# Linear attention and a highway layer: the last tile in three column pieces, and other stores

## The chip, the cores and the metric

The kernel runs on one core of one Trainium2 chip. The metric is the device time in microseconds, as the median of several runs. The engines of a core work side by side and wait for one another through semaphores: TensorE (PE, matmuls into PSUM[...]), VectorE (DVE), ScalarE (ACT), GpSimd (POOL, which works from SBUF alone here) and SyncE (SP), which here only issues transfers. A transfer runs on 16 DMA engines, and whoever needs its data waits for its landing.

## What is computed

For each of 8 batches and 8 heads (576 tokens, 64 dimensions each), q is put through a softmax over its dimensions, k through a softmax over its tokens, and attention is linear: `kv = k_s^T v`, `x = q_s kv`. The heads side by side make 4608 tokens of 512 features, and these go through a highway layer:

```
H = maximum(x @ w_h, 0)
T = 1 / (1 + exp(-(x @ w_t + b_t)))
out = T * H + (1 - T) * x          # float32, 4608 x 512
```

## The kernel before

**Tiles.** The output is cut into 36 tiles of 128 tokens by 512 features. A batch has 9 rows of 64 tokens (token `9p + j`, with p the partition and j the row). Eight rows make four tiles of two rows each, partitions 0 to 63 holding one and 64 to 127 the other; the ninth rows of two batches together make one more tile. So tiles 8, 17, 26 and 35 are ninth-token tiles, and 35 is the last of all. Tiles 0 and 4 are worked in two halves at the start.

**One tile.** `xu` multiplies the transposed exp(q) with the batch's kv (L326, TensorE), which also gives the softmax sums; `rs` and `x` divide (L335, L341, VectorE); `xt` transposes x (L348, TensorE) and `xe` copies it to SBUF as float16 (L355, VectorE or ScalarE). `mh` multiplies it with half of `w_h` less half of the identity (L383), `mt` with `w_t` (L374), into banks `gps` and `tps`. The bias is put into `tps` ahead of that by `bw`: a copy by ScalarE (L364) or a small matmul (L366). Then `th` takes the tanh of half of the gate (L399, ScalarE), `dd` makes `d = max(h, -x/2)` (L403, VectorE), `uu` makes `u = (1 + tanh) d` (L416, VectorE), and `oo` adds x (L432, GpSimd in most tiles). In some tiles, called lifted, GpSimd does `uu` as a plain product (L414) and another sum `ee` (L408), which spares VectorE a step. `st` stores.

**One batch.** `ek` and `eq` take exponentials on ScalarE, `vc` casts v, `kv` multiplies (L258), `kr` and `kn` divide by the sums and write the result to SBUF (L270, L276), `qt` transposes exp(q) (L299) and `qc` copies that out of PSUM (L308). The two banks of pool `ps_x` serve in turn `kv` of a batch and `xu` of every tile but 0 and 4: who comes next waits until VectorE has read what is there.

**Order.** All of it is one list written out by hand, `ORDER`, of some 700 steps (`kind_tile_part`, with `:A`, `:D` or `:P` for the engine where there is a choice). Each engine runs its own steps in the order of this list, and waits where a step's data or buffer isn't there yet. `fill_n` puts n matmuls on zeros where TensorE would stand idle. SP issues loads and stores in list order too, each on one of eight semaphores in turn, so a transfer is issued once the one eight places before it has landed. Weights, bias and inputs come in float32; matmuls are in float16.

**Buffers that the change touches.** Pool `ld` has three landing buffers each for k, q and v. Pool `op` has three buffers for pairs of tiles (`o32`, two tiles stored together) and three for tiles stored alone (`o1`: tiles 8, 17, 26 and 31 to 35). In the last tile, `mt`, `th`, `uu` and `oo` go by two halves of 256 columns, all in one bank `tps`, one buffer `u16` and one buffer `o1`:

```
def columns(i, h):
    return slice(h * DM // 2, (h + 1) * DM // 2) if i == LAST else slice(0, DM)
```

Its four stores are shared between SP and ScalarE's queue. A stored pair writes two rows that are not neighbours, so each packet has 2048 bytes; ninth tokens are stored in two transfers of 64 partitions.

Of the kernel before, what the change touches and what calls it, by code (L numbers as in the profile page):

```python
# [8 lines left out]
FP32 = mybir.dt.float32  # L9
# [7 lines left out]
b_0 b_32 setuppool fill_16_turned setupdve k_0_2 q_0_0 k_0_0 v_0_0 v_0_2 q_0_4 w_h_0 bsplit w_h_2 fill_4_turned bp  # L17
w_t_0 bc eq_0_0 w_t_2 ek_0_3 ek_0_1 v_1_2 ek_0_0 ek_0_2 vc_0_1:D vc_0_0 k_1_0 fill_20_xu_0_0 kv_0_0 qt_0_0 vc_0_2:A
vc_0_3:D k_1_2 qc_0_0:A half kr_0_0 fill_2_xu_0_0 kv_0_1 kn_0_0 kr_0_1 fill_1_xu_0_0 xu_0_0 kn_0_1 eq_0_1 q_1_0 rs_0_0
fill_3_xu_0_1 xu_1_0 x_0_0 xu_0_1 qt_0_1 rs_0_1 rs_1_0 v_1_0 whc_0 xt_0_0 qc_0_1:A x_1_0 whd_1 q_1_4 x_0_1 whc_2 k_2_0  # L20
v_2_0 q_2_0 k_3_0 bw_1 bw_0 fill_5_mh_0_0 xt_0_1 xu_2_0 xe_0_1 rs_2_0 xe_0_0 whd_2 fill_1_mh_0_0 xt_1_0 eq_0_2 whd_0
whd_3 wtc_0 fill_1_mh_0_0 mh_0_0 x_2_0 mh_0_1 xe_1_0 xu_3_0 wtc_2:D mt_0_0 xt_2_0 rs_3_0 dd_0 mt_0_1 mt_1_0 x_3_0
th_0_0 xe_2_0 mh_1_0 uu_0_0 th_1_0 bw_2:A xt_3_0 mh_2_0 dd_1 ek_1_1 uu_1_0 ek_1_0 mt_2_0 xe_3_0:D ek_1_2 dd_2 bw_3
mt_3_0 th_2_0 vc_1_3 vc_1_2 oo_0_0 oo_1_0 ek_1_3 uu_2_0 mh_3_0 th_3_0 oo_2_0 eq_1_0 kv_1_1 dd_3 kr_1_1 vc_1_0:A vc_1_1
fill_2_qt_1_0 qt_1_0 uu_3_0 kn_1_1 kv_1_0 qc_1_0:A kr_1_0 kn_1_0 eq_1_1 st_1_0_1 st_1_0_0 v_3_0 q_3_0 bw_5
fill_1_xu_4_1 xu_4_1 rs_4_1 fill_2_xu_4_0 xu_5_0 x_4_1 rs_5_0 fill_1_xu_4_0 qt_1_1 x_5_0 xu_4_0 bw_4 qc_1_1:A rs_4_0
xt_5_0 x_4_0 fill_2_mh_5_0 xu_6_0 ek_2_2 ek_2_0 xe_5_0:D xt_4_0 mh_5_0 rs_6_0 xe_4_0:D x_6_0 qt_0_2 mt_5_0 dd_5 qc_0_2
oo_3_0 xt_4_1 xu_7_0 th_5_0 xe_4_1:D mh_4_0 rs_7_0 vc_2_2:A vc_2_0 mh_4_1 mt_4_0 mt_4_1 eq_1_2 xt_6_0 qt_1_2 th_4_0
xe_6_0 st_3_0_0 eq_2_0 st_3_0_1 eq_2_1 k_4_0 eq_2_2 v_4_0 uu_5_0 x_7_0 dd_4 kv_2_0 uu_4_0 mh_6_0 kr_2_0 qc_1_2 kn_2_0
bw_6 xt_7_0 qt_2_0 xe_7_0:D dd_6 xu_8_0 mt_6_0 bw_7:A rs_8_0 qc_2_0 mh_7_0 x_8_0 th_6_0 ek_3_0 xu_9_0 uu_6_0 xt_8_0  # L30
mt_7_0 rs_9_0 xe_8_0:D bw_8:A x_9_0 mh_8_0 th_7_0 dd_7 ek_3_2 xt_9_0 oo_5_0 oo_4_0 oo_6_0 mt_8_0 uu_7_0 dd_8 xe_9_0
oo_7_0 xu_10_0 qt_2_1 bw_9:A st_5_0_0 rs_10_0 mh_9_0 x_10_0 th_8_0 st_5_0_1 vc_3_0:A vc_3_2 uu_8_0 mt_9_0 q_4_0 dd_9
xt_10_0 oo_8_0 th_9_0 kv_3_0 xe_10_0:D qc_2_1:A uu_9_0 mh_10_0 kr_3_0 kn_3_0 qt_2_2 eq_3_0 k_5_0 xu_11_0 bw_10 mt_10_0
rs_11_0 qc_2_2:A x_11_0 bw_11:A dd_10 xt_11_0 th_10_0 qt_3_0 xe_11_0:D oo_9_0 xu_12_0 uu_10_0 qc_3_0:A mh_11_0 q_5_0
rs_12_0 oo_10_0 x_12_0 mt_11_0 eq_3_1 dd_11 xt_12_0 bw_12:A xu_13_0 ee_11 xe_12_0:D qt_3_1 th_11_0 rs_13_0 mt_12_0
ek_4_2 x_13_0 v_5_0 uu_11_0:P qc_3_1 xu_14_0 xt_13_0 eq_3_2 mh_12_0 rs_14_0 th_12_0 xe_13_0:D x_14_0 ek_4_0 qt_3_2
mh_13_0 dd_12 bw_13:A xu_15_0 oo_11_0 vc_4_0 uu_12_0 xt_14_0 st_7_0_0 vc_4_2:A mt_13_0 rs_15_0 xe_14_0:D oo_12_0
st_7_0_1 x_15_0 mh_14_0 bw_14:A st_10_0_1 dd_13 xt_15_0 st_10_0_0 kv_4_0 dd_14 xe_15_0 th_13_0 ee_14 mt_14_0 kr_4_0
bw_15:A kn_4_0 ee_13 k_6_0 eq_4_0 qc_3_2 xu_16_0 mt_15_0 rs_16_0 th_14_0 x_16_0 eq_4_1 qt_4_0 xu_17_0 qc_4_0 th_15_0
mh_15_0 rs_17_0 ek_5_2 q_6_0 x_17_0 xt_16_0 qt_4_1 xe_16_0:D bw_16 ek_5_0 dd_15 xu_18_0 xt_17_0 mh_16_0 rs_18_0 x_18_0  # L40
xe_17_0 bw_17:A qc_4_1 xu_19_0 v_6_0 xt_18_0 eq_5_1 mh_17_0 rs_19_0 x_19_0 eq_5_0 mt_16_0 xe_18_0 mt_17_0 th_16_0
qt_5_0 vc_5_2:A st_12_0_0 st_12_0_1 th_17_0 qc_5_0:A eq_5_2 uu_14_0:P uu_13_0:P uu_15_0:P ee_15 dd_16 oo_14_0:D
oo_13_0 vc_5_0 uu_16_0 mh_18_0 dd_17 kv_5_0 oo_15_0 uu_17_0 bw_18 oo_16_0 xt_19_0 kr_5_0 mt_18_0 kn_5_0 xe_19_0
oo_17_0 qt_5_2 xu_20_0 th_18_0 mh_19_0 rs_20_0 bw_19:A bw_20:A qc_5_2 x_20_0 qt_5_1 dd_18 xt_20_0 xu_21_0 qc_5_1:A
mt_19_0 ee_18 rs_21_0 xe_20_0:D x_21_0 ek_6_0 mh_20_0 uu_18_0:P dd_19 xu_22_0 eq_4_2 xt_21_0 th_19_0 rs_22_0 qt_4_2
q_7_0 mt_20_0 ee_19 xe_21_0:D st_14_0_1 bw_21:A x_22_0 st_14_0_0 mh_21_0 eq_6_0 dd_20 k_7_0 qc_4_2 v_7_0 uu_19_0:P
xu_23_0 th_20_0 xt_22_0 mt_21_0 rs_23_0 xe_22_0 x_23_0 oo_18_0 ek_6_2 uu_20_0 xu_24_0 xt_23_0 qt_6_0 rs_24_0 xe_23_0:D
vc_6_0 vc_6_2:A st_8_0_1 mh_22_0 x_24_0 st_16_0_0 dd_21 st_16_0_1 bw_22:A xt_24_0 oo_19_0 kv_6_0 xe_24_0:D th_21_0
qc_6_0 eq_6_2 mt_22_0 ee_21 bw_23:A kr_6_0 kn_6_0 mt_23_0 oo_20_0 dd_22 eq_7_0 xu_25_0 mh_23_0 rs_25_0 uu_21_0:P
th_22_0 x_25_0 eq_7_1 qt_7_0 dd_23 xt_25_0 oo_21_0 xu_26_0 bw_24:A mh_24_0 th_23_0 uu_22_0:P eq_6_1 mt_24_0 st_21_0_0  # L50
uu_23_0:P bw_25:A st_19_0_0 ek_7_2 st_19_0_1 st_8_0_0 th_24_0 eq_7_2 ek_7_0 vc_7_2:A qc_7_0 rs_26_0 x_26_0 xe_25_0:D
dd_24 xu_27_0 xt_26_0 qt_6_1 rs_27_0 x_27_0 mt_25_0 ee_23 xe_26_0:D qc_6_1 xu_28_0 mh_25_0 ee_22 uu_24_0 xt_27_0
rs_28_0 mh_26_0 xe_27_0:D vc_7_0 x_28_0 qt_7_1 dd_26 xt_28_0 bw_26:A kv_7_0 dd_25 th_25_0 xe_28_0 mt_26_0 oo_23_0
oo_22_0 kr_7_0 qc_7_1:A kn_7_0 mh_27_0 oo_24_0 uu_25_0 th_26_0 xu_29_0 mh_28_0 st_23_0_0 uu_26_0 bw_27:A st_23_0_1
rs_29_0 bw_28:A mt_27_0 st_21_0_1 x_29_0 st_17_0_1 dd_27 xu_30_0 st_17_0_0 th_27_0 xt_29_0 mt_28_0 rs_30_0 dd_28
xe_29_0 x_30_0 oo_25_0 oo_26_0 ee_27 qt_7_2 mh_29_0 th_28_0 uu_27_0:P bw_29:A uu_28_0 xt_30_0 xu_31_0 xe_30_0 mt_29_0
oo_28_0 rs_31_0 dd_29 bw_30:A mh_30_0 x_31_0 th_29_0 oo_27_0 xt_31_0 uu_29_0 xu_32_0 xe_31_0 mt_30_0 rs_32_0 oo_29_0
dd_30 bw_31:A mh_31_0 x_32_0 st_28_0_0 th_30_0 st_26_0_0 xt_32_0 st_25_0_1 xu_33_0 xe_32_0 mt_31_0 st_26_0_1 st_28_0_1
mh_32_0 th_31_0 qc_7_2 uu_30_0 rs_33_0 dd_31 x_33_0 bw_32:A qt_6_2 uu_31_0 xt_33_0 xu_34_0 xe_33_0 mt_32_0 dd_32
qc_6_2:A rs_34_0 mh_33_0 x_34_0 th_32_0 bw_33:A xt_34_0 uu_32_0 xu_35_0 xe_34_0 dd_33 mt_33_0 bw_34:A rs_35_0 oo_30_0  # L60
st_30_0_0 oo_31_0 st_31_0_0 oo_32_0 st_25_0_0 st_31_0_1 x_35_0 mh_34_0 st_30_0_1 th_33_0 xt_35_0 uu_33_0 mt_34_0
st_32_0_1 xe_35_0:D st_32_0_0 bw_35:A oo_33_0 dd_34 mh_35_0 th_34_0 mt_35_0 uu_34_0 st_33_0_0 mt_35_1 st_33_0_1 dd_35
th_35_0 oo_34_0 th_35_1 uu_35_0 uu_35_1 oo_35_0:P st_34_0_0 oo_35_1 st_34_0_1 st_35_1_1 st_35_0_0 st_35_0_1 st_35_1_0
# [4 lines left out]
def kernel(  # L68
# [13 lines left out]
    P = 128  # L82
# [7 lines left out]
    ld = pool("ld", 3)  # L90
    ekp = pool("ekp", 2)
# [5 lines left out]
    op = pool("op", 3)  # L97
    PS = bass.MemoryType.PSUM
# [12 lines left out]
    b32 = consts.tile([P, DM], FP32, name="b32")  # L111
# [10 lines left out]
    def once(name, make):  # L122
        if name not in T:
            T[name] = make()
        return T[name]
# [16 lines left out]
    def columns(i, h):  # L142
        return slice(h * DM // 2, (h + 1) * DM // 2) if i == LAST else slice(0, DM)
# [33 lines left out]
    def landing(which, b):  # L177
        return once(f"{which}32{b}", lambda: ld.tile([P, 4, NJ * D], FP32, tag=which, name=f"{which}32_{b}"))
# [115 lines left out]
    def qt(e, b, g):  # L294
        j0, j1 = GROUPS[g]
        t = q_bank(b, g)
        for j in range(j0, j1):
            for kk in range(2):
                nc.tensor.matmul(  # L299
                    t[:, (j - j0) // 2, 2 * kk:2 * kk + 2, (j - j0) % 2],  # L300
                    T[f"qe{b}"][:, j, 2 * kk:2 * kk + 2].rearrange("p c d -> p (c d)"), idh,
                    is_transpose=True, start=True, stop=True, skip_group_check=True)
# [55 lines left out]
    def gate_bank(i):  # L358
        return once(f"tps{i}", lambda: ps_t.tile([P, DM], FP32, tag="tps", name=f"tps_{i}"))

    def bw(e, i):
        t = gate_bank(i)
        if e == "A":
            nc.scalar.copy(t, ball)  # L364
        else:
            nc.tensor.matmul(t, ones, b16, start=True, stop=False, skip_group_check=True)  # L366
# [4 lines left out]
    def mt(e, i, k):  # L371
        cs = columns(i, k)
        for n in parts_of(i, k):
            nc.tensor.matmul(T[f"tps{i}"][:, cs], T[f"xT{i}"][:, n], w16["t"][:, n, cs], start=False,  # L374
                             stop=(n == 3), skip_group_check=True)
# [16 lines left out]
    def th(e, i, h):  # L392
        cs = columns(i, h)
# [96 lines left out]
```

The softmax here doesn't subtract the row's maximum and nothing guards it: scores larger than these inputs give would overflow.

## Time and profile before

| what | value |
|---|---|
| median time of 3 runs | 125.48 us (125.17 to 125.52) |
| span of the profiled run | 123.2 us, TensorE clock 0.989 |
| DMA packets, volume | 19860, 40.08 MB, 325 GB/s over the span |
| HBM read, written | 30.41 MB, 9.44 MB |
| bias by copy (L364) | 27 x 0.593 us on ScalarE |
| bias by matmul (L366) | 9, of 512 columns |
| `oo` on GpSimd (L432) | 34 x about 1.15 us |
| stores of pairs, 256 KB | 28, 10.4 us from issue to landing (median) |
| stores of one tile's half, 128 KB | 14, 3.2 us |

The page gives busy time by engine, then the span in 40 slices with a digit for tenths of busy time, then DMA queues, the chain of work that ended last, and the costliest groups. A matmul's end is modelled, since matmuls are pipelined, so the distance between starts is the better measure of what one costs. In the timeline a row has the start, the duration, engine, line, operation, output and inputs with their shapes, how many, and in square brackets the idle time before it and what ended that.

### The profile page before, as it was taken

The page shows a single profiled execution, that of the slowest core. Times are in us where ns is not written, and L with a number is a line of the kernel's source. Part 1 is how long each engine was busy: PE and PEld are TensorE (multiplying, and loading weights), DVE is VectorE, ACT ScalarE, POOL GpSimd, SP SyncE. Part 2 cuts the span into 40 slices and gives each one's busy share as a digit, 9 for nine tenths or more (in the row PEclk, how much of TensorE's full clock was granted, in tenths as well). Part 3 has the DMA queues.
Part 4 walks back from the last instruction along what each step waited for, and adds up shares of the span by engine and source line. Part 5 has one row for each costly group of instructions (what it writes and reads, how often), then busy time and mean ns, then how long its engine had stood idle before and what let it go on. Part 6 is the DMA issues. An engine that isn't in the chain of part 4 may idle for free.

```text
span 123.2 us, 3484 instructions
## 1 busy us (share of the span) xinstructions
PE 112.3 (91%) x1388; PEld 65.3 (53%) x1388; DVE 99.5 (81%) x233; ACT 97.7 (79%) x148; POOL 72.4 (59%) x73
## 2 busy tenths in 40 slices
PE   5899899998999999899989999999999999999800
PEld 4545544545466466566546566565666655555400
DVE  5505997877988999899879997989999997998740
ACT  4096565996989899699799999999999868777410
POOL 5002002773073256379586996999999999663430
PEclk9999999999999999999999999999999999999995
DMA  3999999999999999999999999999997095499954
GB/s 78 387 394 380 408 396 388 371 379 388 388 390 391 403 392 398 391 407 389 391 391 389 409 397 391 396 402 394 390 349 218 20 205 128 86 232 229 245 128 107
DMA packets 19860, 40.08 MB, mean 325 GB/s; under 512 B 1282, under 2 KB 3586, under 8 KB 19844
## 3 DMA queue, kind: packets, MB, share of 16 engines
q1 hardware_dynamic: 19680, 39.72, 92.3%
q8 instruction: 11, 0.18, 0.6%
q10 hardware_dynamic: 164, 0.14, 0.5%
q14 instruction: 5, 0.04, 0.1%
HBM read 30.41 MB, written 9.44 MB: 324 GB/s over the span
## 4 chain that ended last, share of the span: by engine, by line
PE 41%; DMA 20%; POOL 11%; DVE 9%; ACT 6%; SPq 4%; issue 4%; DVEq 0%; POOLq 0%; ACTq 0%
PE tps L374 13%; PE gps L383 12%; DMA w32t<-in_moe_w_t_dram 11%; POOL o L432 7%; DMA out_dram<-o 6%; PE xu L326 4%; DMA q<-in_q_dram 4%; PE turned L348 4%; PE qps L299 4%; SPq L441 3%; PE kv L258 2%; DVE kvb L276 2%; ACT tps L399 2%; DVE x L341 2%; POOL e L408 2%
## 5 line engine op out<-in xcount | busy, mean ns | idle before, releaser
L432 POOL TENSOR_TENSOR o<-u,x 128x512 f32<-128x512 f16 x25 | 28.8, 1154 | 16.9 <-DVE u L416 14.3
L383 PE MATMUL gps<-w16h,xT 128*128 128x512 f16 x144 | 37.0, 379 | 0.1
L374 PE MATMUL tps<-w16t,xT 128*128 128x512 f16 (+1 forms) x148 | 36.7, 373 | 0.1
L341 DVE TENSOR_TENSOR x<-xu,rs 128x512 f16<-128x512 f32 (+1 forms) x38 | 25.0, 658 | 0.7
L403 DVE SCALAR_TENSOR_TENSOR d<-x,gps 128x512 f16<-128x512 f16 x36 | 24.1, 673 | 1.1 <-PE gps L383 1.0
L245 POOL CAST v<-v 128x1152 f16<-128x1152 f32 (+1 forms) x10 | 9.9, 1000 | 23.6 <-DMA v<-in_v_dram 17.8
L416 DVE SCALAR_TENSOR_TENSOR u<-tps,d 128x512 f16<-128x512 f32 (+1 forms) x27 | 17.9, 669 | 3.7 <-ACT tps L399 2.4
L286 ACT ACTIVATE qe<-q 128x1024 f16<-128x1024 f32 (+1 forms) x24 | 19.9, 843 | 0.2 <-DMA q<-in_q_dram 0.2
L399 ACT ACTIVATE tps<-tps 128x512 f32<-128x512 f32 (+1 forms) x27 | 15.4, 571 | 5.7 <-PE tps L374 5.4
L383 PEld LDWEIGHTS <-xT 128*128 128x128 f16 x144 | 12.9, 98 | 12.5 <-DVE xT L355 0.9
L374 PEld LDWEIGHTS <-xT 128*128 128x128 f16 x148 | 13.3, 98 | 11.7 <-issue 0.4
L239 ACT ACTIVATE ek<-k 128x1152 f16<-128x1152 f32 (+1 forms) x20 | 18.6, 968 | 0.0
L364 ACT COPY tps<-ball 128x512 f32<-128x512 f32 x27 | 15.9, 593 | 1.2 <-DVE u L416 1.1
L326 PE MATMUL xu<-kvb,eq 128*128 128x130 f16 (+1 forms) x160 | 14.7, 224 | 1.2 <-DVE kvb L276 1.1
L348 PE MATMUL turned<-idh,x 128*128 128x128 f16 x144 | 14.3, 219 | 0.4 <-ACT xT L355 0.3
L326 PEld LDWEIGHTS <-eq 128*128 128x128 f16 (+1 forms) x160 | 10.0, 100 | 7.9 <-DVE kvb L276 2.1
L348 PEld LDWEIGHTS <-x 128*128 128x128 f16 x144 | 10.2, 98 | 6.3 <-DVE x L341 2.4
L408 POOL TENSOR_TENSOR e<-d,x 128x512 f16<-128x512 f16 x10 | 11.5, 1159 | 2.8 <-DVE d L403 2.8
L414 POOL TENSOR_TENSOR u<-th,d 128x512 f16<-128x512 f16 x10 | 11.5, 1160 | 1.4 <-DVE rs L335 1.0
L355 ACT COPY xT<-turned 128x512 f16<-128x512 f16 (+1 forms) x18 | 10.0, 563 | 2.9 <-PE turned L348 2.5
L308 ACT COPY eq<-qps 128x1024 f16<-128x1024 f16 (+1 forms) x11 | 9.9, 901 | 2.8 <-PE qps L299 2.7
L299 PE MATMUL qps<-idh,qe 128*128 128x128 f16 x144 | 12.0, 219 | 0.0
(50 smaller groups left out, 118.7 us busy)
## 6 DMA issues: line engine op xcount, KB each, us to landing
out_dram<-o SPq DMA_DIRECT2D x28, 256.0 KB, 10.4
k<-in_k_dram SPq DMA_DIRECT2D x6, 1152.0 KB, 14.5
v<-in_v_dram SPq DMA_DIRECT2D x6, 1152.0 KB, 14.7
q<-in_q_dram SPq DMA_DIRECT2D x6, 1152.0 KB, 14.4
k<-in_k_dram SPq DMA_DIRECT2D x4, 576.0 KB, 9.5
v<-in_v_dram SPq DMA_DIRECT2D x4, 576.0 KB, 7.9
out_dram<-o SPq DMA_DIRECT2D x14, 128.0 KB, 3.2
q<-in_q_dram SPq DMA_DIRECT2D x2, 640.0 KB, 10.6
```

What stands on the lines that cost most here:

```text
L239: nc.scalar.activation(t[:, :, c:c + n].rearrange("p j c d -> p c j d"), T[f"k32{b}"][:, c:c + n].rearrange("p c (j d) -> p c j d", j=NJ), ...
L286: nc.scalar.activation(t[:, j0:j1].rearrange("p j c d -> p c j d"), T[f"q32{b}"].rearrange("p c (j d) -> p c j d", j=NJ)[:, :, j0:j1], AF.Exp)
L299: nc.tensor.matmul(t[:, (j - j0) // 2, 2 * kk:2 * kk + 2, (j - j0) % 2], T[f"qe{b}"][:, j, 2 * kk:2 * kk + 2].rearrange("p c d -> p (c d)" ...
L326: nc.tensor.matmul(dst, T[f"eq{b}_{jp // 2}"][:, jp % 2, n], kvb[b % NKV][:, hh, kk], start=True, stop=True, skip_group_check=True)
L341: nc.vector.tensor_mul(t[:, k0:k1], sums(i, k)[:, :, :, 0:64], T[f"rs{i}_{k}"][:, 0:k1 - k0].unsqueeze(3).to_broadcast([P, k1 - k0, 4, D]))
L348: nc.tensor.matmul(t[:, n], T[f"x{i}"][:, dims(n)], idh, is_transpose=True, start=True, stop=True, skip_group_check=True)
L374: nc.tensor.matmul(T[f"tps{i}"][:, cs], T[f"xT{i}"][:, n], w16["t"][:, n, cs], start=False, stop=(n == 3), skip_group_check=True)
L383: nc.tensor.matmul(t, T[f"xT{i}"][:, n], w16["h"][:, n], start=(n == 0), stop=(n == 3), skip_group_check=True)
L399: nc.scalar.activation(src, src, AF.Tanh, scale=0.5)
L403: nc.vector.scalar_tensor_tensor(t, T[f"x{i}"], -0.5, T[f"gps{i}"], op0=ALU.mult, op1=ALU.max)
L416: nc.vector.scalar_tensor_tensor(t[:, cs], T[f"tps{i}"][:, cs], 1.0, T[f"d{i}"][:, cs], op0=ALU.add, op1=ALU.mult)
L432: eng.tensor_add(t[:, cs], T[f"u{i}"][:, cs], T[f"{'e' if lifted(i) else 'x'}{i}"][:, cs])
```

## The change

The diff has four parts, and a new `ORDER` around them. The pieces with banks and buffers of their own are to let one engine work on a piece while another still works on the next; the stores are to need fewer transfers and fewer packets; the further buffers are to let loads and sums start without waiting for an earlier transfer.

- The last tile is cut into pieces of 256, 128 and 128 columns. Each has a gate bank of its own (in `ps_t`, `ps_g` and `ps_x`), a `u16` buffer and an output buffer of its own. The middle piece is added on GpSimd. Each piece is stored by one transfer of 128 partitions, so three instead of four.
- Rows are dealt to tiles in another way, so that a stored pair holds neighbouring rows: 4096 contiguous bytes per packet.
- Ninth tokens are stored by one transfer of 128 partitions, since the destination now spans both batches.
- q has four landing buffers instead of three; tiles that are stored alone have a pool of five buffers, which the bias row `b32` borrows at the start.

The new list also moves single steps to other engines: 12 tiles are lifted instead of 10, 30 biases are copies instead of 27 (of the last tile's three pieces one is a copy), and some PSUM copies change between ScalarE and VectorE. Some stores go to ScalarE's queue. Load order at the start is k, v, q instead of k, q, k, v.

```diff
     ld = pool("ld", 3)
+    ldq = pool("ldq", 4)
...
     op = pool("op", 3)
+    o1p = pool("o1p", 5)
...
-    b32 = consts.tile([P, DM], FP32, name="b32")
+    b32 = o1p.tile([P, DM], FP32, tag="o1", name="b32")
...
     def columns(i, h):
-        return slice(h * DM // 2, (h + 1) * DM // 2) if i == LAST else slice(0, DM)
+        return (slice(0, 2 * P), slice(2 * P, 3 * P), slice(3 * P, DM))[h] if i == LAST else slice(0, DM)
...
                 nc.tensor.matmul(
-                    t[:, (j - j0) // 2, 2 * kk:2 * kk + 2, (j - j0) % 2],
+                    t[:, (j - j0) % 2, 2 * kk:2 * kk + 2, (j - j0) // 2],
...
-    def gate_bank(i):
-        return once(f"tps{i}", lambda: ps_t.tile([P, DM], FP32, tag="tps", name=f"tps_{i}"))
+    def gate_bank(i, h=0):
+        cs = columns(i, h)
+        make = (lambda: ps_t.tile([P, DM], FP32, tag="tps", name=f"tps_{i}"),
+                lambda: ps_g.tile([P, DM], FP32, tag="gps", name=f"tps_{i}_1"),
+                lambda: ps_x.tile([P, 2, DM], FP32, tag="xu", name=f"tps_{i}_2")[:, 0])[h]
+        return once(f"tps{i}_{h}", make)[:, 0:cs.stop - cs.start]
...
     def uu(e, i, h):
         cs = columns(i, h)
-        t = once(f"u{i}", lambda: dp.tile([P, DM], FP16, tag="u16", name=f"u16_{i}"))
+        t = T[f"u{i}_{h}"] = dp.tile([P, DM], FP16, tag="u16", name=f"u16_{i}_{h}")
...
         if mate(i) is None:
-            t = once(f"o{i}", lambda: op.tile([P, DM], FP32, tag="o1", name=f"o32_{i}"))
+            t = T[f"o{i}_{h}"] = o1p.tile([P, DM], FP32, tag="o1", name=f"o32_{i}_{h}")
...
     def st(e, i, h, r):
         bs, jp = tiles[i]
-        b = bs[r % len(bs)]
         cs, rows = columns(i, h), slice(NP * r, NP * r + NP)
-        eng = nc.scalar if i == LAST and r else nc.sync
-        dst = out[b * S:(b + 1) * S, cs].rearrange("(p j) n -> p j n", j=NJ)
+        eng = nc.scalar if e == "A" else nc.sync
+        dst = out[bs[0] * S:(bs[-1] + 1) * S, cs].rearrange("(p j) n -> p j n", j=NJ)
         if mate(i) is not None:
-            eng.dma_start(dst[:, 2 * jp + r - 2:2 * jp + r + 1:2], T[f"oo{i - 1}"][rows])
+            eng.dma_start(dst[:, 2 * (jp + r) - 2:2 * (jp + r)], T[f"oo{i - 1}"][rows])
         elif len(bs) == 1:
-            eng.dma_start(dst[:, 2 * jp + r], T[f"o{i}"][rows, cs])
-        else:
-            eng.dma_start(dst[:, 8], T[f"o{i}"][rows, cs])
+            eng.dma_start(dst[:, 4 * (jp // 2) + 2 * r + jp % 2], T[f"o{i}_{h}"][rows])
+        else:
+            eng.dma_start(dst[:, 8], T[f"o{i}_{h}"][:, 0:cs.stop - cs.start])
```

The parts of the two lists that the prediction speaks of (TensorE's steps and what stands among them):

```diff
-kv_3_0 xe_10_0:D qc_2_1:A uu_9_0 mh_10_0 kr_3_0 kn_3_0 qt_2_2 eq_3_0 k_5_0 xu_11_0
+kv_3_0 xe_10_0:D v_4_0 bw_10:A k_4_0 mh_10_0 qc_2_1:A kr_3_0 st_5_0_0 kn_3_0 eq_3_0 q_4_0 qt_2_2 dd_10 xu_11_0
...
-kv_4_0 dd_14 xe_15_0 th_13_0 ee_14 mt_14_0 kr_4_0 bw_15:A kn_4_0 ee_13 k_6_0 eq_4_0 qc_3_2 xu_16_0
+kv_4_0 bw_15:A st_10_0_0 dd_14 oo_12_0 k_6_0 xt_15_0 eq_4_0 qt_3_2 kr_4_0 mt_14_0 kn_4_0 ee_13 qc_3_2:A xe_15_0:D th_14_0 xu_16_0
...
-mt_34_0 st_32_0_1 xe_35_0:D st_32_0_0 bw_35:A oo_33_0 dd_34 mh_35_0 th_34_0 mt_35_0 uu_34_0 st_33_0_0 mt_35_1 st_33_0_1 dd_35
-th_35_0 oo_34_0 th_35_1 uu_35_0 uu_35_1 oo_35_0:P st_34_0_0 oo_35_1 st_34_0_1 st_35_1_1 st_35_0_0 st_35_0_1 st_35_1_0
+mt_34_0 xe_35_0 dd_34 st_25_0_0 oo_33_0 bw_35_0 bw_35_2 th_34_0 mh_35_0 st_32_0_0:A uu_34_0
+st_33_0_1 mt_35_0 dd_35 st_33_0_0 mt_35_1 oo_34_0 mt_35_2 th_35_0 th_35_1 th_35_2 uu_35_0 uu_35_1 oo_35_0 st_34_0_0
+st_34_0_1:A oo_35_1:P uu_35_2 st_35_1_0:A st_35_0_0 oo_35_2 st_35_2_0
```

## The prediction

> **What bounds the kernel now.** I read the page's busy shares first, then the slices, then the chain of waits, then the timeline of the stretches that the chain names.
>
> ```profile
> PE 112.3 (91%) x1388; PEld 65.3 (53%) x1388; DVE 99.5 (81%) x233; ACT 97.7 (79%) x148; POOL 72.4 (59%) x73
> ...
> PE   5899899998999999899989999999999999999800
> ...
> DMA  3999999999999999999999999999997095499954
> ```
>
> TensorE is the first candidate, but these ends are modelled, so I took start-to-start distances: 0.216 us for a matmul of 512 columns (0.86 for four in the chain), 0.056 for 128, and summed them. Real work is 93.7 us, `fill` matmuls 11.1, idle 11.3. From 20.0 us, when the second half of `w_t` has landed (19.23 in the chain) and is cast, to the last matmul at 116.29, TensorE has only about 6 us of idle and 1.7 of fills in 96. So **the order on TensorE sets the time from 20 to 116.3**, and what follows it is a bare tail of 6.9 us. DMA is full to 91 us, but k, v and q arrive ahead of need: the trace has the last v landing at 91.17 and its matmuls at 95.5. The few idle stretches worth naming are in the chain:
>
> ```profile
> 48.12 0.69 DVE u L416
> 48.81 0.10 DVE rz L270
> 48.93 0.42 DVE kvb L276
> 49.36 0.44 DVE kvb L276
> 49.80 0.05 issue
> 49.85 0.41 PE xu L326 x4
> ```
>
> Here `kv_3` has ended at 48.17, but VectorE does `uu_9` (0.69) before it reads the bank for `kr_3` and `kn_3`; `xu_11` waits until 49.85, 0.56 of idle. A like wait ahead of `xu_16` is 0.51 (kv to 61.25, `mt_14`, then nothing until 62.76). The others over 0.2 us lie at 27.6 (0.75), 31.0, 37.2 and 67.8. The tail is in the timeline:
>
> ```profile
> 115.42 1.04 PE L374 MATMUL tps<-w16t,xT 128*128 128x256 f16 x8
> ...
> 116.01 0.68 DVE L403 SCALAR_TENSOR_TENSOR d<-x,gps 128x512 f16<-128x512 f16 x1
> 116.55 0.77 ACT L399 ACTIVATE tps<-tps 128x256 f32<-128x256 f32 x2 [1.24 <-PE tps L374]
> 116.84 1.15 POOL L432 TENSOR_TENSOR o<-u,x 128x512 f32<-128x512 f16 x1 [1.45 <-DVE d L403]
> 117.41 0.76 DVE L416 SCALAR_TENSOR_TENSOR u<-tps,d 128x256 f16<-128x256 f32 x2 [0.72 <-ACT tps L399]
> 118.09 0.76 DVE L432 TENSOR_TENSOR o<-u,x 128x256 f32<-128x256 f16 x2
> 118.88 1.17 ACTq L445 DMA_DIRECT2D out_dram<-o  x2
> 119.22 1.19 SPq L445 DMA_DIRECT2D out_dram<-o  x2
> ```
>
> The halves of the last tile gain nothing from being halves: half 0 is multiplied by 115.85, yet its tanh starts at 116.55, after half 1; and the first `uu` starts at 117.41, after both tanhs (117.32), though its `dd` was ready at 116.69. `oo_34` too starts at 116.84, not at the 116.09 when its `uu` ends: the trace has a store landing at 116.68, that of `o31`, whose buffer it takes (three buffers). The last store is issued at 119.86 and lands at 122.09; the closing barrier takes 1.03.
>
> **What the Trainium skill says.** "PSUM — Partial Sum Buffer", PSUM bank collisions: two engines may not touch one bank in the same partitions at once, so guarding is by bank, not by address. That is what the two late starts above show. "SBUF — State Buffer", Door 1: partitions 0 to 63 reach only half of the 16 DMA ports. The trace agrees late in the run: from 98 to 103 us, with only 64-partition stores, most packets of 2048 bytes take about 165 ns and 200 GB/s move, against 84 ns beside loads. "DMA: Bandwidth & Descriptors", Anatomy of one DMA: a fixed 2 us or so lies mostly in the confirmation. The last store here takes 2.22 from issue. "TensorE: Matmul & The Clock Gate", Wait — 56ns, not 53.3ns: 55.6 and 215.7 ns between warm matmuls of 128 and 512 columns, as measured above.
>
> **The change, part by part.**
>
> *Last tile.* TensorE's own time is the same (4 x 0.110 + 8 x 0.056 = 0.88). With separate banks `th_35_0` need not wait for the other pieces, nor `uu_35_0` for the later tanhs. VectorE then sets the pace: `dd_35` ends at 116.69 as now, `uu_35_0` starts there (not 117.41). Two 256-column operations start 0.34 apart here; 128 columns I put at 0.2 apart and 0.29 long (512 take 0.689, 256 take 0.420, a line through both). So `uu_35_1` 117.03, `oo_35_0` 117.23, `uu_35_2` 117.57 to 117.86, `oo_35_2` to 118.15. ScalarE: `th_34` ends at 115.31, then the store of `o32` that is moved to its queue (0.5), then tanhs of 0.37, 0.26 and 0.26 from 115.9: all done by 116.8, in time. GpSimd's piece `oo_35_1` (0.29 by length to 0.4) follows `oo_34`, which now starts at 116.1 and ends at 117.3, so 117.7. SP: store of `o34` at 117.3, `st_35_0_0` at 117.85, `st_35_2_0` at 118.45, each some 0.55; plus 2.22 makes 120.67 for 122.09: **-1.42**. Without SP's queue it would be -1.7.
>
> *A new wait.* `o35_2` takes, as eleventh tile in a ring of five, the buffer of `o32`, so `oo_35_2` waits for both stores of `o32`, one of which now stands behind `th_34` on ScalarE, issued near 115.3. Stores issued from 114 to 116 land after 2.5 to 3.8 us. At 2.5 to 2.8 it lands by 118.1, hidden by the path above; at 3.8 at 119.1, which makes the end 121.67 (-0.42). I take the short end, since one store transfer fewer is ahead of it. Only `st_35_2_0` is queued behind.
>
> *TensorE work.* After 20 us seven bias matmuls (1.51) become five and the two short ones (1.25): **-0.26**. Three more bias copies of 0.59 go to ScalarE, and its copies change places with VectorE's; both have 20% slack and I cost them nothing, hidden by matmuls.
>
> *Order.* `uu_9` goes to GpSimd, so `kr_3` can start at 48.2 and `kn_3` end at 49.25, as TensorE gets to `xu_11`: **-0.56**. Between `kv_4` and `xu_16` now stand `xt_15` (0.22) and `qt_3_2` (0.11): **-0.33**. Against that, `mt_3` moves behind `mh_3`, so ScalarE does `eq_1_0` before `th_3`; VectorE's `uu_3` and then `kn_1_1` follow, and `kv_1_0` waits for that bank, as the chain has it at 28.32 now: 0.2 to 0.5 later, say **+0.3**. And `mh_35` takes the bank of `gps_34`, since a piece of the last tile has taken the other one: it waits for `dd_34` (ending near 114.84) where TensorE comes at 114.7: **+0.15**. The count of fills after 20 us is 8 in both.
>
> *Stores.* 4096 bytes per packet from the same 64 partitions meet the same half of the ports: nothing. Ninth tokens (3 earlier tiles) in one transfer from 128 partitions free three issues of 0.6 on SP, which waits for GpSimd there: nothing. The fourth q buffer lets loads start earlier, but none is waited for on the path: nothing. k_4 and v_4 now stand behind stores of tiles 5 and 7; they landed at 52 and 55 for use at 60.6, so that is hidden too.
>
> Sum: -1.42 - 0.26 - 0.56 - 0.33 + 0.3 + 0.15 = -2.1. The whole order is new, and I have walked only the places where it idles now; half of a stall like those above, +0.2, is my estimate for what appears elsewhere. 125.48 - 1.9 = **123.6**.
>
> **Rivals.**
> 1. *Only the tail pays*: stalls go elsewhere. For it: DVE and ACT at 80% leave little to shift. 125.48 - 1.4 = 124.1.
> 2. *The buffer wait takes the place of the bank wait*: the store of `o32` lands late, DMA being at 0.94 from 110 to 116. Tail -0.42, bias -0.26, and half of what the order and the reserve leave (-0.56 - 0.33 + 0.3 + 0.15 + 0.2 = -0.24): 124.7.
> 3. *Slower*: the new order misfits in the dense stretch. For it: there is no idle there now to absorb a late operand. With four new stalls like that at 49 us (4 x 0.56 = 2.2), no order gain, and the +0.45 of the two late starts against -1.42 and -0.26: 126.5. Against it: around the old stalls the new order has more work between a bank's last use and its next.
> 4. *Better*: 31.0, 37.2 and 67.8 (0.27, 0.31, 0.20) close as well and the tail takes -1.7: 122.6.
>
> **How the numbers follow.** Forecast 0.45, rival 1 0.20, rival 2 0.12, slower 0.14, better 0.09. The range 122.5 to 125.2 leaves out the slower case and a little below. Faster by over 0.3% (below 125.1): the forecast, rival 1, better and most of rival 2, 0.82; same 0.04; slower 0.14.
>
> **What would show it.** The first tanh of tile 35 starting before its last matmul, the first `uu` about when `dd_35` ends, `oo_34` right behind its `uu`; `xu_11` and `xu_16` without a gap; `kv_1_0` late by 0.2 to 0.5. Wrong would be: the last matmul later than about 116.5, or `oo_35_2` waiting for a DMA.

## The result, and the profile after

The changed kernel takes **126.92 us** (126.54 to 128.66 in four runs) where the kernel before takes 125.5 beside it: a ratio of 1.011, with a 95% interval of 1.0077 to 1.0143. It is slower, and the forecast of 123.6 with its range to 125.2 was wrong. Two executions in a slow state are left out of every ratio and difference here: the 128.66 (the other three have a median of 126.78), and one of 395 us of a later kernel, the one with the loads first. The span of the profiled run is 124.8 us instead of 123.2.

Read the page of the kernel after in the same order as that of before. These are its lines for TensorE and for DMA in 40 slices (3.12 us each) and the volume moved; the volume of the kernel before stands below them:

```profile
PE   5999979978999999999979929999999999999920
...
DMA  3999999999999998999999999999999674139985
GB/s 118 360 391 389 405 394 384 371 380 385 390 401 404 388 378 206 346 391 406 395 388 391 406 399 393 391 407 401 389 354 213 187 148 85 37 66 242 270 253 147
```

```profile
GB/s 78 387 394 380 408 396 388 371 379 388 388 390 391 403 392 398 391 407 389 391 391 389 409 397 391 396 402 394 390 349 218 20 205 128 86 232 229 245 128 107
```

Two digits stand out. TensorE has a 2 in the slice that begins at 71.8 us, where before it has a 9. And the volume falls to 206 and 346 GB/s between 46.8 and 53.0 us, in a stretch that runs at 390 to 400 before. The DMA digits there are still 8 and 9: busy time hides what the volume shows, because the packets of 64-partition stores take longer there (4096 bytes in about 318 ns between 46.8 and 49.9 us, against 159 beside loads). The two are one event, 25 us apart. The list of waits (engine, line, what was waited for: us in total, how often, longest) names its end:

```profile
PE kv L261 <- POOL v L248: 2.4, 1, 2.4
...
POOL e L415 <- DVE o L440: 2.2, 1, 2.2
...
DVE o L440 <- DMA out_dram<-o: 1.9, 2, 1.2
```

Such a wait counts from the modelled end of the matmul before; by the distances between starts, as all gaps of TensorE below are counted, this one is 2.59. `kv_5` waits for GpSimd's half of the cast of v (`vc_5_0`); GpSimd had stood at the sum `ee_16`, whose buffer `oo_14` on VectorE had still to read; and `oo_14` had waited for a store to land, whose buffer it takes. The chain of waits puts times to it and shows where it began (start, duration, what):

```profile
44.81 1.16 POOL o L440
...
45.99 0.47 SPq L449
...
72.57 0.34 POOL e L415
...
73.67 1.16 POOL v L248
...
74.87 0.80 PE kv L261 x63
```

L449 is a pair's store. SyncE's own rows show what stands behind it (L189 loads k and v):

```profile
34.61 13.31 SPq L449 DMA_DIRECT2D out_dram<-o  x4
48.01 0.55 SPq L189 DMA_DIRECT2D v<-in_v_dram  x1
48.61 0.74 SPq L189 DMA_DIRECT2D k<-in_k_dram  x1
```

For 13.3 us SyncE issued four stores and nothing else. Two were out by 38.2; then `st_7_0_0` stood at the head, which waits for GpSimd's `oo_7` until 45.97 (the longest single wait of SyncE for GpSimd is 7.7 us; before it is 5.3), and behind it v_4 and k_4. In the kernel before these two were issued some 8 us earlier:

```profile
39.47 0.64 SPq L186 DMA_DIRECT2D k<-in_k_dram  x1
40.54 2.38 SPq L186 DMA_DIRECT2D v<-in_v_dram  x1
```

So the loads already under way ran out, and DMA had only 64-partition stores from 47 to 50 us. What was not moved then, (395 - 206 + 395 - 346) GB/s x 3.12 us = 0.74 MB, is 1.9 us of transfer at 395 GB/s. Since DMA is full up to 91 us, nothing wins that back, and what was issued behind v_4 comes late: k_4 lands at 58.29 instead of 51.99, q_4 at 61.91 (59.22), v_5 at 70.95 (68.20; these 2.7 us are more than the 1.9, and the rest is not accounted for), and `st_7_0_1`, issued behind v_5, at 71.61. That last is the store that `oo_14` waits for. The first two hold up ScalarE:

```profile
58.31 2.22 ACT L242 ACTIVATE ek<-k 128x1152 f16<-128x1152 f32 x2 [0.97 <-DMA k<-in_k_dram]
...
61.94 1.06 ACT L289 ACTIVATE qe<-q 128x1024 f16<-128x1024 f32 x1 [0.30 <-DMA q<-in_q_dram]
```

ScalarE works in order, so what stands behind these exponentials is late too: TensorE has a gap of 0.32 inside `kv_4`, which needs the second part of k_4, and one of 0.81 at `qt_4_0` (63.30), which needs the copy `qc_3_2` right behind the exponential of q_4.

The tail did what it was meant to do, except at its end (timeline of the kernel after):

```profile
117.28 0.56 ACTq L451 DMA_DIRECT2D out_dram<-o  x1
...
118.15 1.05 PE L382 MATMUL tps<-w16t,xT 128*128 128x256 f16 x12
118.50 0.68 DVE L410 SCALAR_TENSOR_TENSOR d<-x,gps 128x512 f16<-128x512 f16 x1
118.66 1.15 POOL L440 TENSOR_TENSOR o<-u,x 128x512 f32<-128x512 f16 x1 [0.78 <-DVE u L423]
118.79 0.71 ACT L406 ACTIVATE tps<-tps 128x256 f32<-128x256 f32 x3 [0.99 <-PE tps L382]
119.31 0.62 DVE L423 SCALAR_TENSOR_TENSOR u<-tps,d 128x256 f16<-128x256 f32 x2
...
121.19 0.84 SPq L453 DMA_DIRECT2D out_dram<-o  x2
121.21 0.29 DVE L440 TENSOR_TENSOR o<-u,x 128x128 f32<-128x128 f16 x1 [0.75 <-DMA out_dram<-o]
```

The first tanh starts at 118.79, before the last matmul's end at 119.04; the first `uu` at 119.31, right behind `dd_35` (to 119.18). But `oo_35_2` waits 0.75 for the store of `o32` in the first row, issued at 117.28 on ScalarE's queue and landed at 121.13. From the last matmul to the last landing (123.80) it is 4.76 us, 5.80 before.

### The profile page after: what moved, and what is told of

It reads as the page before. It is cut to its first block, busy times and chain, and to the rows that moved or that the text cites. A ratio compares the mean times of both kernels' runs of the same rounds, so it can differ in the third digit from the quotient of the medians.

```text
span 124.8 us, 3490 instructions
## 1 busy us (share of the span) xinstructions
PE 111.7 (90%) x1388; PEld 65.4 (52%) x1388; DVE 97.5 (78%) x232; ACT 98.1 (79%) x152; POOL 77.1 (62%) x78
## 4 chain that ended last, share of the span: by engine, by line
PE 36%; DMA 25%; POOL 12%; issue 8%; ACT 6%; DVE 5%; SPq 4%; POOLq 0%; DVEq 0%
DMA k<-in_k_dram 16%; PE tps L382 12%; PE gps L391 12%; DMA out_dram<-o 9%; PE xu L329 4%; POOL o L440 4%; POOL u L421 4%; PE turned L351 4%; POOL e L415 3%; ACT qe L289 2%; PE qps L302 2%; SPq L189 2%; PE kv L261 2%; SPq L449 2%; ACT tps L406 1%
## 5 line engine op out<-in xcount | busy, mean ns | idle before, releaser
L440 POOL TENSOR_TENSOR o<-u,x 128x512 f32<-128x512 f16 (+1 forms) x24 | 26.8, 1124 | 34.3 <-DVE u L423 31.4
L382 PE MATMUL tps<-w16t,xT 128*128 128x512 f16 (+2 forms) x152 | 37.0, 368 | 0.5 <-ACT w16t L213 0.5
L423 DVE SCALAR_TENSOR_TENSOR u<-tps,d 128x512 f16<-128x512 f32 (+2 forms) x26 | 16.7, 647 | 4.6 <-ACT tps L406 3.3
L372 ACT COPY tps<-ball 128x512 f32<-128x512 f32 (+1 forms) x30 | 17.5, 587 | 1.2 <-DVE u L423 1.2
L406 ACT ACTIVATE tps<-tps 128x512 f32<-128x512 f32 (+2 forms) x26 | 14.1, 550 | 4.4 <-PE tps L382 4.3
L415 POOL TENSOR_TENSOR e<-d,x 128x512 f16<-128x512 f16 x12 | 13.9, 1156 | 2.3 <-DVE o L440 2.2
L421 POOL TENSOR_TENSOR u<-th,d 128x512 f16<-128x512 f16 x12 | 13.8, 1156 | 0.0
L311 ACT COPY eq<-qps 128x1024 f16<-128x1024 f16 (+1 forms) x15 | 12.0, 797 | 2.3 <-PE qps L302 2.2
L440 POOL TENSOR_TENSOR o<-u,e 128x512 f32<-128x512 f16 x11 | 12.6, 1156 | 0.5
```

The source lines that it names most:

```text
L372: nc.scalar.copy(t, ball[:, cs])
L382: nc.tensor.matmul(gate_bank(i, k if i == LAST else 0), T[f"xT{i}"][:, n], w16["t"][:, n, cs], start=False, stop=(n == 3), skip_group_chec ...
L415: nc.gpsimd.tensor_add(T[f"e{i}"], T[f"d{i}"], T[f"x{i}"])
L421: nc.gpsimd.tensor_mul(t, T[f"th{i}"], T[f"d{i}"])
L440: eng.tensor_add(t[:, 0:w], T[f"u{i}_{h}"][:, 0:w], T[f"{'e' if lifted(i) else 'x'}{i}"][:, cs])
```

## The experiments

Spans between fixed points show where the kernels differ. All numbers but the medians are from the traces, one execution each; "tail" is from the end of the last matmul to the last landing, and that end is taken as its start plus the measured distance of such matmuls, 0.11 us for 256 columns and 0.056 for 128. "Loads first" alone has no row, because its profile is that of the 395 us.

| kernel | median us | `kv_1_0` to `kv_5` | `kv_5` to last matmul | tail |
|---|---|---|---|---|
| before | 125.48 | 44.19 | 43.78 | 5.80 |
| after | 126.78 | 46.54 | 44.17 | 4.76 |
| after, four pair buffers | 125.42 | 45.25 | 44.01 | 4.99 |
| after, loads first, store on SyncE | 124.82 | 44.28 | 44.18 | 5.32 |
| after, loads first, cast first | **123.25** | 42.95 | 44.19 | 4.84 |
| the same, six buffers | 123.42 | 42.99 | 44.18 | 4.76 |
| the same as two rows up, store earlier | 123.76 | 42.94 | 44.19 | 6.14 |
| before, loads late | 126.43 | 44.91 | 43.87 | 5.67 |
| before, neighbouring rows | 124.84 | 44.08 | 43.87 | 5.73 |
| old list, new code | 123.85 | 44.20 | 44.37 | 4.06 |
| the same, bank later | 125.98 | 44.07 | 44.02 | 6.35 |
| the same, bank later, tile 9 lifted | 125.59 | 43.79 | 44.02 | 6.34 |
| the same, and six buffers | 123.62 | 44.02 | 43.93 | 4.52 |

### Is it the two loads?

**Loads first.** In the changed list, `v_4_0` and `k_4_0` go ahead of the stores:

```diff
-st_7_0_0 ... st_5_0_1 ... v_4_0 ... k_4_0
+v_4_0 k_4_0 st_7_0_0 ... st_5_0_1
```

> The changed kernel with the loads v_4 and k_4 ahead of the stores st_7_0_0 and st_5_0_1 in the list, as they stood before the change; nothing else. Theory L (late loads): SP stood from 38.2 to 46.0 us waiting for GpSimd's sum of tile 7 with v_4 and k_4 behind it, DMA ran low from 46 to 50 us, and everything after landed some 2.1 to 2.7 us later (v_5 70.95 for 68.2), which gives the 2.59 us gap of TensorE ahead of kv_5. Expected: no dip of DMA, v_5 near 68.3, the gap under 0.5, about 124.4 (-2.5). Rival O (the new order misfits on the engines in many places, no matter when loads land): the gap closes at most in part and the time stays above 126.

Measured: 124.58 us, ratio 0.9935 to before (0.9913 to 0.9957). That is 2.2 us less than the changed kernel, for moving two issues, and the time agrees with the theory of the loads. Whether the gap at `kv_5` closed, as that theory has it, is seen in a run further below.

**Four pair buffers.** If the harm came only through the buffer that `oo_14` waits for, one more would end it:

```diff
-    ldq = pool("ldq", 4)
+    ldq = pool("ldq", 3)
...
-    op = pool("op", 3)
+    op = pool("op", 4)
```

> The changed kernel with four buffers for stored pairs instead of three (the room comes from q's landing buffers, three again instead of four); loads stay late. Theory S (the way by which lateness reaches TensorE is a buffer: oo_14 waits until 71.6 us for the landing of st_7_0_1, then ee_16 and vc_5_0 stand behind it on GpSimd): without that wait vc_5_0 can start once v_5 is there, near 71.0, the gap ahead of kv_5 falls from 2.59 to under 0.5, about 124.6. If loads being late is what counts by itself (L without S), vc_5_0 is still late and the gap stays over 1.5: 126 or more. Rival O: 126.5.

Measured: 125.42 us (ratio 1.0005, 0.9981 to 1.0029). The gap at `kv_5` falls from 2.59 to 1.29, which neither theory had; the low stretch of DMA is still there (234 and 287 GB/s) and v_5 still lands at 71.3. GpSimd's rows:

```profile
71.27 1.15 POOL L415 TENSOR_TENSOR e<-d,x 128x512 f16<-128x512 f16 x1 [1.28 <-DVE o L440]
72.38 1.14 POOL L248 CAST v<-v 128x1152 f16<-128x1152 f32 x1
```

So the buffer is the path by which 1.3 us of the stall came. The other 1.29 is not the late v_5: `oo_14` now runs without a wait for a store, but `ee_16` waits until `oo_14` has had its turn on VectorE, and the cast stands behind `ee_16`; the same 1.29 comes back below, where v_5 lands at 68.58. What the late k_4 and q_4 cost stands earlier, and it is unchanged here: 0.32 in `kv_4` and 0.80 at `qt_4_0`.

**The reverse, in the kernel before.**

```diff
-k_4_0 ... v_4_0 ... st_5_0_0 ... st_5_0_1
+st_5_0_0 ... st_5_0_1 v_4_0 k_4_0
```

> The kernel before with v_4 and k_4 moved behind the two stores of tiles 4 and 5 (st_5_0_0, st_5_0_1), all else as before. L: SP waits for GpSimd with the loads behind it, DMA runs low near 46 to 48 us, v_5 lands over a microsecond later than 68.2 and kv_5 waits: 126.5 to 128. O: no change, 125.5.

Measured: 126.43 us (ratio 1.0076, 1.0055 to 1.0098), slower as expected, but by another way: here the stores are ready early, SyncE stands less, and no slice from 40 to 62 us is under 388 GB/s. What costs is the landing of k_4 at 56.07 instead of 51.99 (chain of waits):

```profile
41.66 14.42 DMA k<-in_k_dram
...
56.10 1.16 ACT ek L239
...
57.57 0.48 ACT tps L399
...
59.66 1.02 PE tps L374 x4
```

There too the exponential of k_4, late by 4 us, pushes a tanh and a bias behind it, and TensorE idles 0.33 and 0.60 there. "Landed at 52 for use at 60.6" left out that ScalarE's exponentials come in between.

### What holds kv_5 once the loads are early

**Loads first, with the store of `o32` on SyncE.**

```diff
-st_32_0_1 ... th_34_0 mh_35_0 st_32_0_0:A
+st_32_0_1 st_32_0_0 ... th_34_0 mh_35_0
```

> The changed kernel with two edits in its list: v_4 and k_4 are issued ahead of the stores st_7_0_0 and st_5_0_1 (as in the run before, 124.58), and st_32_0_0 goes out on SyncE right behind st_32_0_1 instead of on ScalarE's queue behind th_34. Theory L (the loads of batch 4 that stand behind stores cost 2.3 us, and the store of o32 that lands late costs another 0.7): v_5 lands near 68.3 and not 70.95, the gap of TensorE at kv_5 is under 0.5 instead of 2.59, no slice of the DMA between 45 and 51 us is under 320 GB/s, oo_35_2 no longer waits for a DMA (0.75 before), and the time is 123.9 (123.6 to 124.2). Rival D (only the two loads matter; another wait takes the place of that of oo_35_2, for instance the queue of SyncE at the end): 124.4 to 124.7. Rival B (the low DMA stretch comes from the packets of 4096 bytes, not from the order of the loads): a slice under 260 GB/s stays.

Measured: 124.82 us (ratio 0.9958, 0.9938 to 0.9977), so not below loads first alone. Two parts of theory L hold: no slice from 45 to 51 us is under 389 GB/s, and v_5 lands at 68.58. Rival B, the packets of 4096 bytes, is out. Two parts fail. At the end, rival D: `oo_35_2` waits 0.32 instead of 0.75, but SyncE has one more store in its queue, and its last two issues come at 119.13 and 119.91, with `oo_35_2` done at 118.74; the tail is 5.32 instead of 4.76. The Trainium skill has this in "DMA: Bandwidth & Descriptors", Issuing engines are not separate DMA queues: spreading transfers over engines saves only the sequencer's issue time. That is what ScalarE's queue had saved here. And at `kv_5` there is still a gap of 1.29, as with four pair buffers. So what the early loads win is the gaps in `kv_4` and at `qt_4_0`, which are gone (`kv_1_0` to `kv_5` is 0.97 shorter than with four pair buffers), and the wait of `oo_14` for a store; v_5 itself, landing 2.7 us sooner, wins nothing here. GpSimd's rows of this run show what is left:

```profile
67.80 1.15 POOL L415 TENSOR_TENSOR e<-d,x 128x512 f16<-128x512 f16 x1
70.23 1.15 POOL L415 TENSOR_TENSOR e<-d,x 128x512 f16<-128x512 f16 x1 [1.28 <-DVE o L440]
71.33 1.15 POOL L248 CAST v<-v 128x1152 f16<-128x1152 f32 x1
```

The data is there at 68.58 and GpSimd is free at 68.95, but `ee_16` is next in its order and waits for `oo_14`; the cast stands behind it. In the kernel before the cast ran to 72.37, though v_5 had landed at 68.20, and TensorE came to `kv_5` at 72.42, so the cast had no slack at all:

```profile
70.76 1.61 POOL L245 CAST v<-v 128x1152 f16<-128x1152 f32 x1
```

Here TensorE comes at 71.23, 1.2 us sooner, thanks to the new list; and waits until 72.52.

**Cast first.** From the list with the loads first:

```diff
-ee_16 vc_5_0 oo_13_0 kv_5_0
+vc_5_0 ee_16 oo_13_0 kv_5_0
```

> The changed kernel with v_4 and k_4 ahead of the stores (as in the run with 124.58) and one more edit: vc_5_0, GpSimd's half of the cast of v_5, stands ahead of ee_16 instead of behind it. In the run with the loads first and st_32_0_0 on SyncE, v_5 lands at 68.58, GpSimd is free at 68.95, but ee_16 waits for oo_14 until 70.23 and the cast runs from 71.33 to 72.47, with kv_5 at 72.52 behind a gap of 1.29. Theory Q (the rest of the stall is the order on GpSimd's queue, not the data): the cast runs from about 69.0 to 70.2, the gap at kv_5 falls under 0.3, and the time to 123.6 (123.3 to 123.9). Rival W (the stores and loads themselves are late there; oo_14, which waits for the landing of a store at 69.2, holds up the next step, ee_16, oo_15 or mt_18, by as much): the gap moves within 4 us behind kv_5 and the time stays at 124.4 to 124.8.

Measured: **123.25 us** (122.96 to 123.64), ratio 0.9849 to before (0.9813 to 0.9885): 1.3 less than loads first alone (1.1 when each is set against the kernel before that ran beside it). GpSimd's rows:

```profile
68.00 1.16 POOL L415 TENSOR_TENSOR e<-d,x 128x512 f16<-128x512 f16 x1
69.10 1.15 POOL L248 CAST v<-v 128x1152 f16<-128x1152 f32 x1
70.87 1.16 POOL L415 TENSOR_TENSOR e<-d,x 128x512 f16<-128x512 f16 x1 [0.62 <-DVE o L440]
```

The cast runs as soon as GpSimd is free, `kv_5` starts at 71.53 behind a gap of 0.09, and no wait of like size follows within 4 us. By these times the cast needs v_5 before 69.1, so this gain is to be had only with the loads early. So two things cost the change its gain: 2.2 us for two loads behind a store, and 1.1 to 1.3 us for one cast behind a sum. Without these two the new list and code beat the kernel before by 1.9 to 2.0.

### The tail and the buffers of single tiles

**Old list, new code.** The changed code with the kernel before's list; only the steps of the last tile are the new ones, and the second steps of the ninth-token stores, which have nothing left to do, are out.

```diff
-ORDER: the new list
+ORDER: the list of before up to mt_34_0, without st_8_0_1 st_17_0_1 st_26_0_1; then
+mt_34_0 st_32_0_1 xe_35_0:D st_32_0_0 bw_35_1:A oo_33_0 dd_34 bw_35_0 bw_35_2 mh_35_0 th_34_0 mt_35_0 uu_34_0
+st_33_0_0 mt_35_1 st_33_0_1 mt_35_2 dd_35 oo_34_0 th_35_0 th_35_1 th_35_2 uu_35_0 ... (as in the new list)
```

> The code of the changed kernel (rows dealt anew, 4096-byte packets, one transfer for ninth tokens, five single buffers, four q buffers, the last tile in three pieces) run by the list of before; only the second stores of tiles 8, 17 and 26 are gone and the last steps are those of the new last tile. L and O agree that the new list alone costs time: 125.5 less about 1.0 for the tail (the distance from last matmul to last landing is 4.76 after, 5.80 before): about 124.4. If the new stores or buffers themselves cost time: 125.5 or more.

Measured: 123.85 us (ratio 0.9877, 0.9837 to 0.9916), better than expected. TensorE is no faster than before; the gain is in the tail, 4.06 instead of 5.80. So it is the new list, and not the new code, that makes the changed kernel slow: between the two lie 2.9 us. Here `o32` was stored early enough, and `oo_35_2` starts at 118.11, right behind its `uu`.

**Bank later.** `mh_35` has a gap of 0.44 in that run, since the middle piece has taken the other bank.

```diff
-bw_35_1:A oo_33_0 dd_34 bw_35_0 bw_35_2 mh_35_0 th_34_0
+oo_33_0 dd_34 bw_35_0 bw_35_2 mh_35_0 th_34_0 bw_35_1:A
```

> The changed kernel's code with the list of the kernel before and the new steps of the last tile (the run before with 123.85), in which the bias of the middle piece of tile 35 is copied behind th_34 instead of ahead of dd_34. The middle piece then takes the bank that gps_34 leaves, and mh_35 needs only dd_33. Theory: the gap of TensorE at mh_35 (0.44) falls to about 0.1 and the time to 123.5. Rival: the copy behind th_34 makes mt_35_1 wait as long as mh_35 did, so the last matmul ends no earlier: 123.85 within 0.2.

Measured: 125.98 us, 2.1 slower. Neither theory saw that coming. The gap is gone and the last matmul comes 0.5 sooner after `kv_1_0`; but in this program `o35_2` has the buffer that the middle piece of the same tile was just stored from, instead of that of `o32`, and waits for that store (issued at 118.29, landed at 120.96):

```profile
118.29 0.64 ACTq L453 DMA_DIRECT2D out_dram<-o  x1
121.14 0.29 DVE L440 TENSOR_TENSOR o<-u,x 128x128 f32<-128x128 f16 x1 [2.96 <-issue]
```

Why the buffers were given out otherwise after a step on another engine moved, no run tells.

**Tile 9 lifted**, on top of it:

```diff
-kv_3_0 ... uu_9_0 ... kr_3_0 kn_3_0 ... xe_11_0:D oo_9_0
+kv_3_0 ... kr_3_0 kn_3_0 ... xe_11_0:D uu_9_0:P ee_9 oo_9_0
```

> The list and code of e7_bank_later with tile 9 lifted: its u is a plain product on GpSimd (uu_9 behind xe_11, with the sum ee_9 on VectorE), so that kr_3 and kn_3 start as soon as kv_3 has ended. Theory (the gap of 0.56 at xu_11 is worth its whole length, as the prediction has it): the gap falls to under 0.1 and the time by 0.5 against e7_bank_later, to about 123.0. Rival G (the gap moves to a later step, as in the changed kernel, where qt_2_2 and xt_11 wait 0.81 in its place): the same time as e7_bank_later within 0.2, with new gaps within 3 us of xu_11.

Measured: 125.59 us, 0.4 less than without; the wait at the end is the same. The gap at `xu_11` falls from 0.56 to 0.28, not to under 0.1, so about half of what was expected there.

**Six buffers**, on top of that:

```diff
-    ldq = pool("ldq", 4)
+    ldq = pool("ldq", 3)
...
-    o1p = pool("o1p", 5)
+    o1p = pool("o1p", 6)
```

> The old list with the code of the change, tile 9 lifted and the bank taken later (the run with 125.59), with six buffers for tiles that are stored alone instead of five, and three for q instead of four to make room. In the run with 125.59 oo_35_2 got the buffer that the middle piece of the same tile had just been stored from, and waited 2.9 us for that store to land. Theory: with six buffers it gets that of o31, stored long before; it runs right behind uu_35_2, the last store is issued near 118.4 instead of 121.2, and the time is 123.3 (123.0 to 123.6), so 2.3 less. Rival: SyncE's queue, which then issues all last stores at once, sets the end: 123.9 or more.

Measured: 123.62 us (ratio 0.9876, 0.984 to 0.9912), 2.0 less. `oo_35_2` starts at 117.90, right behind its `uu`, and the last store is issued at 118.44. That shows the buffer as the cause. Yet it is hardly better than the old list with the new code, although TensorE is 0.6 shorter: the tail takes 0.46 of it back.

**Six buffers for the best version**, on top of "cast first":

```diff
-    ldq = pool("ldq", 4)
+    ldq = pool("ldq", 3)
...
-    o1p = pool("o1p", 5)
+    o1p = pool("o1p", 6)
```

> The kernel of the run with 123.25 (loads first, cast first) with six buffers for tiles stored alone instead of five, and three for q instead of four to make room: oo_35_2 no longer needs the buffer of o32, whose second store, issued at 113.97 on ScalarE's queue, lands only at 118.26 and holds oo_35_2 from about 117.3 to 118.34. Theory of the prediction (the buffer is the wait that matters): oo_35_2 runs at 117.3 and the time falls by 0.5 to 0.9, to 122.4 to 122.8. Rival (the queue: st_35_0_0 on SyncE also waits until 118.33, for the same landing, since it reuses the semaphore of that store; the last store behind it is issued no earlier): 123.25 within 0.2, with oo_35_2 early and the last two stores issued as before.

Measured: 123.42 us (ratio 0.9863, 0.9822 to 0.9904), no gain, as the rival had it:

```profile
117.18 0.29 DVE L440 TENSOR_TENSOR o<-u,x 128x128 f32<-128x128 f16 x1
118.14 0.83 SPq L453 DMA_DIRECT2D out_dram<-o  x2
```

`oo_35_2` is done at 117.47, but SyncE's last two stores still begin at 118.14, just after the store of `o32` landed at 118.08, whose semaphore the first of them reuses.

**The store earlier.**

```diff
-mt_34_0 xe_35_0 ... th_34_0 mh_35_0 st_32_0_0:A
+mt_34_0 st_32_0_0:A xe_35_0 ... th_34_0 mh_35_0
```

> The kernel of the run with 123.25 with one step moved: st_32_0_0 on ScalarE's queue stands ahead of xe_35_0 instead of behind th_34_0, so it is issued about 1.2 us earlier (112.8 instead of 113.97). Theory: it lands about 0.7 earlier, both oo_35_2 and st_35_0_0 wait less, and though xe_35 is 0.2 later the time falls by 0.3 to 0.6, to 122.7 to 122.9. Rival (stores land in the order in which the DMA works them off, whoever issues them; the landing moves by less than 0.3): 123.25 within 0.2, or slower by the 0.2 of xe_35.

Measured: 123.76 us (ratio 0.9893, 0.9837 to 0.9948): no gain. Issued at 112.44, it lands at 117.77, 5.3 us later, where it took 4.3 when issued at 113.97 and landed at 118.26. That is between the theory and the rival. The profiled execution is this kernel's longest (124.98), so its tail of 6.14 is not typical.

### The packets

**Neighbouring rows alone**, in the kernel before:

```diff
-t[:, (j - j0) // 2, 2 * kk:2 * kk + 2, (j - j0) % 2]
+t[:, (j - j0) % 2, 2 * kk:2 * kk + 2, (j - j0) // 2]
...
-dst[:, 2 * jp + r - 2:2 * jp + r + 1:2]
+dst[:, 2 * (jp + r) - 2:2 * (jp + r)]
```

> The kernel before with one edit: rows are dealt to tiles so that a stored pair holds neighbouring rows, and its packets have 4096 bytes instead of 2048. Theory (packet size is worth nothing, as predicted): 125.4 within 0.3, with some 4000 packets fewer on the queues than without. Rival P (half as many packets relieve the DMA): faster by 0.5 or more, 124.9. Rival Q (packets of 4096 bytes from 64 partitions move fewer bytes a second): slower by 0.5 or more, and a slice under 320 GB/s ahead of 90 us.

Measured: 124.84 us beside 125.42 (ratio 0.9957, 0.9937 to 0.9977). That is 0.6 faster, which is what rival P had, and not the theory. The trace does not show where: from `kv_1_0` to the last matmul 87.95 us (87.97 before), tail 5.73 (5.80), with 18068 packets instead of 19860. But the profiled execution (125.63) is the longest of this kernel's twenty, 0.8 above their median, so where the 0.6 lies stays open.

## Why the prediction was wrong

- **The step that failed: "k_4 and v_4 now stand behind stores of tiles 5 and 7; they landed at 52 and 55 for use at 60.6, so that is hidden too".** It was put at nothing and cost 2.2 us. SyncE's queue was taken as short, though the store at its head waits for GpSimd until 46. The use of k_4 was taken to be the matmul at 60.6, though ScalarE's exponential comes before that: ScalarE stood for 0.97 until k_4 landed at 58.29, and TensorE lost about 1.0 by it and by the late q_4 (0.32 in `kv_4`, 0.81 at `qt_4_0`). And only these two loads were looked at, though DMA is full and so passes a delay on to later transfers: `st_7_0_1` landed at 71.61, and the wait of `oo_14` for it cost another 1.3 at `kv_5`. "k, v and q arrive ahead of need" rested on the last v alone (91.17 for 95.5).
- **The gains of the order were added up on TensorE alone.** Their place came out right: `xu_11` has 0.07 instead of 0.56, `xu_16` 0.05 instead of 0.51. But `qt_2_2` (0.35) and `xt_11` (0.46, before 0.11) took the first back, `qt_4_0` (0.81, for the late k_4 and q_4) the second; that last gap is gone with the loads first. What TensorE then has gained by 71 us it loses at `kv_5`, whose cast stands behind `ee_16`: 1.3 us.
- **"I take the short end"** for the store of `o32`: it landed 3.85 us after its issue, nearer 3.8 than 2.5 to 2.8, and the tail gained 1.04 instead of 1.42. "Only `st_35_2_0` is queued behind" was also short: `st_35_0_0` waits for the same landing through its semaphore, so another buffer alone is worth nothing.
- **Right:** separate banks let the tail start early (the whole new tail is worth 1.74 with the old list), and `mh_35` waits 0.11 (0.15). The wait ahead of `kv_1_0` is longer by 0.52 (1.27 for 0.75), but `kv_1_0` starts at 28.3 in both traces, so the +0.3 was not paid. Neighbouring rows, put at nothing, gain 0.6 in the kernel before, and no trace shows where. Three q buffers with six single ones do as well as four with five (123.42 beside 123.25). The bias matmuls, the lifted tiles other than 9, the one-transfer stores of ninth tokens and the load order at the start were not tried alone.
- Rival 3, slower at 126.5, was near in its number, but not with four stalls of one size: one of 2.59 at `kv_5` leads, with 0.81 at `qt_4_0`, 0.81 around `xt_11` and 0.32 in `kv_4`. With the two steps mended the kernel takes 123.25, near the forecast of 123.6; that is partly luck, for the tail gains 0.96 there instead of 1.42, and the +0.3 ahead of `kv_1_0` is not paid.

## What to carry to other kernels

Before you call a moved load hidden, look at what stands ahead of it in its issuing queue and when that can go; a store that waits for an engine blocks every load behind it, and where DMA is full the lost time moves on to later transfers, here to a store whose buffer was needed again. Take that slack from the tightest batch, through every engine between landing and matmul, not from the last one. An order that saves time on one engine pays only up to the next point where another engine's order, a buffer or a semaphore sets the time, so walk all queues up to that point.

## What the runs showed of the hardware

Packets of 4096 bytes from 64 partitions are no faster than those of 2048 when they are alone on DMA: from 102 to 104 us of the kernel after, 49 to 50 of them a microsecond make 200 to 205 GB/s with the engines fully busy, and from 100 to 102 us of the kernel before 93 to 100 packets of 2048 bytes make 199 to 205. Beside loads, about 390 GB/s go through (47 to 50 us with the loads first and the store on SyncE). And one issue on SyncE, mostly 0.6 us, took up to 1.9 with several stores under way (113.13 to 115.02 in the run with the store earlier); the sum that it stores had ended at 112.41, and what it waits for is not shown.
